# A linear-attention scan and a rational feed-forward layer on one core: units of one batch, register scales, and half of the denominators summed by DMA

## The chip, the cores and the metric

The kernel runs on one core of a Trainium2 chip. The engines are TensorE (PE in the profile, with PEld for its weight loads), VectorE (DVE), ScalarE (ACT), GpSimd (POOL) and SyncE (SP, which here only issues DMAs). The metric is device time in microseconds (us); the median of several runs is compared.

## The reference

Inputs q, k, v and f_logit have the shape [batch 4, heads 8, tokens 768, dim 48]. The first half is a recurrence with a gate for each key dimension; the second half is a feed-forward layer with a rational activation on 3072 tokens of width 8 x 48 = 384.

```python
f = 1 / (1 + exp(-f_logit))
for t in range(768):
    state = f[:, :, t, :, None] * state + outer(k[:, :, t], v[:, :, t])
    y[:, :, t] = q[:, :, t] @ state
x = y laid out as [3072, 384]
h = x @ w_in                                    # d_ff 2048
P = a0 + a1*h + a2*h*h + a3*h*h*h
Q = 1 + |b0|*|h| + |b1|*h*h + 1e-6
out = (P / Q) @ w_out
```

## The kernel before

The work is cut into 12 units of 256 tokens. A unit is two blocks of 128 tokens, one of each of two batches; a block stands on 64 partitions, two successive tokens (index i) to a partition. Twelve units are six chunks of 128 tokens times two pairs of batches, and the state of a pair is carried from chunk to chunk.

For the attention part of unit n the steps are, by their names in the code: `ld` (loads of f, k, q on SP's queue, of v with a cast to bf16 on POOL's queue, L185 to L195, two DMAs for an array, one per batch), `ef` and `ls` (exp and ln on ScalarE, L279 and L284: the log of the gate), `cs` (its running sum over the tokens by matmuls with triangular matrices, L294), `A` (exp of plus and minus that sum, L304 and L306, the one for q with a per-partition bias), `xa` (product with q and k on VectorE, L311), `T` and `Te` (transposes on TensorE and their copy out of PSUM, L322 and L330), `sc` and `mk` (scores, and their masking on VectorE, L343 and L351), `vm` (a copy of parts of v on POOL, L358), `ya` (the product with the carried state, and the next state in PSUM, L364 to L400), `yb` (scores times v, L364), `ye` (copy of y to the tile xT, L420), `ae` (exp of the last log sum, L425) and `st` (new state on VectorE, L429).

For the feed-forward part a unit has 16 tiles (m) of 128 hidden features by 256 tokens. The steps are: `h` (w_in products, L438), `hy` (copy of h to bf16 on ScalarE, L452), `sq` on VectorE (L456) or `sa` on ScalarE (L460) for h squared, `ab` (absolute value, L464), the denominator's sum either by `u` (two matmuls with the identity, L472, followed by `ln`, L480), or by `zd` (a DMA with addition issued on POOL, L489) or `zv` (VectorE, L485), both followed by `lz` (ln, L496). `ex` (L504) makes exp(-ln Q) = 1/Q. The numerator is `p1` (L509), `p2` (L514), `pm` (L519), then `ta` (a DMA with addition issued on POOL, L523) or `tv` (the same on VectorE, L527); `gm` (L532) multiplies numerator and 1/Q. `o` (L539) is the w_out product, `oe` (L554) its copy out of PSUM, `so` (L548) the store, two DMAs.

The features are scaled beforehand so that the denominator is c*(|h'| + h'*h') + 1: the factor sig[0] enters through the bias of `A` for q, and c is sig[2], a per-partition pointer in `ln` and `lz`.

Every engine and every DMA queue runs its instructions in program order, and the program order is written out by hand in the string ORDER (L19 to L104): some 800 steps, one after the other, with PSUM slots @0 to @3 (two banks each) named where a step opens one. A step waits for its data and for the free slot; all that is behind it on the same engine waits too. The load tiles have three buffers each.

Before the change the units differ: units 0 and 1 have all denominators by `u` and use `tv`; `sa` takes 48 of the 192 tiles of h squared, `zd` 40 and `zv` 24 of the denominators' tiles, `u` 128.

Of the kernel before, what the change touches and what calls it, by code (L numbers as in the profile page):

```python
# [19 lines left out]
cz 1; ld 0 v; ab_; ld 0 q 2 4; cz 0; ld 0 f 2 4; cz 2; cb; ld 0 f 0 2; wi 0 4; ld 0 k 2 4; fa  # L20
ld 0 k 0 2; cz 3; fb; ld 0 q 0 2; ef 0 2 4; ls 0 2 4; vm 0 0; ef 0 0 2; ld 1 f; vm 0 1; ls 0 0 2; ca
wi 4 16; cs 0 2 4 @0; cc; cs 0 0 2 @1; A 0 0 2 4; A 0 1 0 2; xa 0 0 2 4; A 0 1 2 4; A 0 0 0 2
xa 0 1 2 4; ld 1 k; xa 0 1 0 2; T 0 2 4 @1; xa 0 0 0 2; ld 1 q; Te 0 2 4; ld 1 v; T 0 0 2 @0
sc 0 1 @1; Te 0 0 2; ef 1; ld 2 f; mk 0 1; sc 0 0 @0; ya 0 @2 @3; ls 1; mk 0 0; yb 0 2 4; ae 0
cs 1 @1; st 0; yb 0 0 2; A 1 1; A 1 0; ye 0; h 0 0 4 @2; hy 0 0 4; h 0 4 8 @1; wo 4 8; wo 12 16
h 0 12 16 @2; hy 0 4 8; xa 1 1; ld 2 k; wo 0 4; h 0 8 12 @3; sq 0 0 8; wo 8 12; hy 0 12 16; ld 2 q
ab 0 0 8; hy 0 8 12; xa 1 0; u 0 0 4 @2; ab 0 8 16; T 1 @3; vm 1 0; ln 0 0 4; p1 0 0 8; ld 2 v
u 0 4 8 @1; Te 1; ef 2; ld 3 f; p2 0 0 8; sc 1 1 @3; vm 1 1; ln 0 4 8; sc 1 0 @2; mk 1 1; ls 2
ya 1 @1 @0; mk 1 0; ex 0 0 8; cs 2 @3; sq 0 8 16; yb 1; A 2 1; pm 0 0 8; u 0 12 16 @2; ye 1
p1 0 8 16; ae 1; A 2 0; h 1 0 4 @1; tv 0 0 8; ln 0 12 16; ld 3 k; h 1 12 16 @3; hy 1 0 4; p2 0 8 16  # L30
gm 0 0 8; h 1 4 8 @2; hy 1 12 16; pm 0 8 16; u 0 8 12 @1; hy 1 4 8; xa 2 1; h 1 8 12 @3; ln 0 8 12
tv 0 8 16; o 0 0 0 4 @2; ex 0 8 16; ab 1 0 8; o 0 1 0 4; sq 1 0 8; o 0 0 4 8; ld 3 q; hy 1 8 12
o 0 1 4 8; xa 2 0; u 1 0 4 @1; gm 0 8 16; T 2 @3; ld 3 v; ln 1 0 4; st 1; o 0 1 8 12; o 0 1 12 16
Te 2; ef 3; ld 4 f; vm 2 0; u 1 4 8 @0; vm 2 1; ls 3; sq 1 8 16; sc 2 0 @3; ln 1 4 8; sc 2 1 @1
ld 4 k; o 0 0 8 12; mk 2 0; o 0 0 12 16; ex 1 0 8; cs 3 @0; mk 2 1; ld 4 q; ab 1 8 16; A 3 1
ya 2 @1 @3; p1 1 0 16; A 3 0; vm 3 0; oe 0 0 2 s; yb 2; ld 4 v; xa 3 1; u 1 12 16 @0; ae 2; ye 2
so 0 0 2; p2 1 0 16; u 1 8 12 @2; ef 4; ld 5 f; vm 3 1; ln 1 12 16; h 2 12 16 @1; pm 1 0 8; ls 4
ld 5 k; st 2; h 2 0 4 @0; hy 2 12 16; tv 1 0 8; ln 1 8 12; cs 4 @3; ld 5 q; xa 3 0; h 2 4 8 @1
hy 2 0 4; gm 1 0 8; sa 2 0 4; h 2 8 12 @2; ld 5 v; pm 1 8 16; hy 2 4 8; o 1 0 0 4 @0; hy 2 8 12
ab 2 0 8; o 1 1 0 4; vm 4 1; tv 1 8 16; A 4 0; o 1 0 4 8; vm 4 0; ld 6 f; sa 2 4 8; T 3 @2  # L40
p1 2 0 16; A 4 1; o 1 1 4 8; ld 6 k; ex 1 8 16; xa 4 0; u 2 4 8 @1; Te 3; u 2 0 4 @3; ld 6 q
ln 2 4 8; gm 1 8 16; sc 3 1 @2; ln 2 0 4; sc 3 0 @1; mk 3 1; o 1 0 8 12; ef 5; o 1 1 8 12; mk 3 0
ex 2 0 8; o 1 1 12 16; ya 3 @2 @3; xa 4 1; ld 7 f; pm 2 0 8; ef 6; yb 3; ae 3; ls 5; T 4 @1; ld 7 k
# [69 lines left out]
def kernel(  # L113
# [14 lines left out]
    C = 128  # L128
# [91 lines left out]
    def const_b():  # L220
        make_identity(nc, ident)
# [372 lines left out]
```

## Time and profile before

| | |
|---|---|
| median of 3 runs | 247.41 us (247.39 to 249.63) |
| span of the profiled execution | 244.1 us |
| busy PE, DVE, ACT, POOL | 214.6, 210.6, 204.8, 62.1 us |
| first and second write of xT (start) | 26.85, 42.70 us |
| DMA packets, bytes moved | 61342, 37.94 MB |
| landing of one accumulating DMA of 512 KB (median) | 6.1 us (gall), 6.2 us (z) |

The page gives the span of one profiled execution, from the first to the last instruction, not that execution's own time; the median is of other runs and contains 3.3 us more. Busy time is the union of an engine's instructions; TensorE's are pipelined, so its busy share says little about its peak. In the list of groups a line names source line, engine, operation, tiles written and read, shapes, count, busy time and mean duration, then the idle time before such instructions and what ended it. A landing is the time from the issue of a DMA to its completion.

### The profile page before, as it was taken

Reading aid. Unit: us, or ns where it says so; the run is one execution under the profiler, and the core shown is the slowest. Engines: PE = TensorE matmul, PEld = TensorE weight load, DVE = VectorE, ACT = ScalarE, POOL = GpSimd, SP = SyncE. Lnnn points to the kernel's source line nnn. Section 1 sums busy time; section 2 is a strip of 40 time slices with the busy share of each in tenths; the row PEclk is TensorE's granted clock in tenths of the full one; section 3 lists DMA queues with packets and bytes.
Section 4 is the critical chain, followed back from the end, with each engine's and each line's share of the span. In section 5 each row is a group of like instructions: output and inputs, shape, how many; then the busy total and the mean of one; then the engine's idle time right before and its main releaser. Section 6 shows DMA issues by size and latency. Waiting matters only on the chain.

```text
span 244.1 us, 7193 instructions
## 1 busy us (share of the span) xinstructions
PE 214.6 (88%) x3144; PEld 146.9 (60%) x3144; DVE 210.6 (86%) x233; ACT 204.8 (84%) x213; POOL 62.1 (25%) x98
## 2 busy tenths in 40 slices
PE   0228787999998999997999999999999999999991
PEld 0115564765774868665668577668568658666550
DVE  7427179999999999999979999999999998899740
ACT  2422568989999899999799999999999999999930
POOL 7953201500400344233071032242122102004110
PEclk9999997999999999999999999999999999999997
DMA  6999999980799999999989999678529746606972
GB/s 82 217 199 198 204 196 221 208 131 0 127 208 204 166 239 169 201 200 220 161 161 165 232 179 172 101 153 131 105 74 172 145 97 118 121 3 129 199 145 64
DMA packets 61342, 37.94 MB, mean 155 GB/s; under 512 B 52096, under 2 KB 57600, under 8 KB 61312
## 3 DMA queue, kind: packets, MB, share of 16 engines
q0 software_dynamic: 19424, 18.62, 49.3%
q1 hardware_dynamic: 41888, 18.88, 40.1%
q8 instruction: 24, 0.39, 0.7%
q14 instruction: 6, 0.05, 0.1%
HBM read 25.17 MB, written 4.72 MB: 122 GB/s over the span
## 4 chain that ended last, share of the span: by engine, by line
PE 42%; ACT 18%; DMA 13%; DVE 13%; SPq 7%; issue 5%; DVEq 0%; ACTq 0%
PE op L539 15%; PE hp L438 13%; DMA fn<-in_f_logit_dram 8%; SPq L194 7%; DMA gall<-hy 5%; PE u L472 5%; ACT hy L452 4%; DVE gall L532 3%; ACT qi L504 3%; ACT lq L480 3%; PE y L364 2%; PE tp L322 2%; DVE h L456 2%; DVE gall L509 2%; PE sc L343 2%
## 5 line engine op out<-in xcount | busy, mean ns | idle before, releaser
L438 PE MATMUL hp<-xT,w_in_sb 128*128 128x256 bf16 x576 | 67.9, 273 | 1.7 <-ACT xT L420 1.4
L539 PE MATMUL op<-w_out_sb,gall 128*128 128x384 bf16 x384 | 68.4, 326 | 0.9 <-DVE osb L554 0.7
L438 PEld LDWEIGHTS <-w_in_sb 128*128 128x128 bf16 x576 | 55.4, 98 | 11.5 <-issue 2.1
L452 ACT CAST hy<-hp 128x1024 bf16<-128x1024 f32 x48 | 48.5, 1021 | 5.7 <-PE hp L438 5.4
L539 PEld LDWEIGHTS <-gall 128*128 128x128 bf16 x384 | 36.3, 98 | 25.5 <-DVE gall L532 1.2
L504 ACT ACTIVATE qi<-lq 128x2048 bf16<-128x2048 f32 (+1 forms) x25 | 46.5, 1871 | 0.2
L523 POOL DMA_DIRECT2D gall<-hy x21 | 19.5, 960 | 83.6 <-ACT hy L452 14.8
L480 ACT ACTIVATE lq<-u,sig 128x1024 f32<-128x1024 f32 x32 | 35.4, 1134 | 1.2 <-PE u L472 1.1
L532 DVE TENSOR_TENSOR gall<-gall,qi 128x2048 bf16<-128x2048 bf16 (+1 forms) x25 | 29.5, 1182 | 4.1 <-DMA gall<-hy 4.0
L351 DVE TENSOR_TENSOR scm<-sc,mask 128x1024 bf16<-128x1024 f32 x24 | 28.7, 1217 | 1.6 <-PE sc L343 1.6
L519 DVE TENSOR_TENSOR gall<-gall,h 128x2048 bf16<-128x2048 bf16 (+1 forms) x25 | 29.3, 1181 | 0.0
L194 POOL DMA_DIRECT2D vn<-in_v_dram x24 | 18.8, 801 | 27.0 <-issue 20.3
L456 DVE TENSOR_TENSOR h<-hy 128x2048 bf16<-128x2048 bf16 (+1 forms) x19 | 22.2, 1167 | 2.1 <-ACT hy L452 2.1
L294 PE MATMUL cs<-lsp,Ui 128*128 128x384 bf16 (+1 forms) x39 | 11.6, 359 | 12.5 <-ACT lsp L284 12.5
L358 POOL COPY vmp<-vn 128x128 bf16<-128x128 bf16 x24 | 10.7, 483 | 44.0 <-PE y L364 27.9
L279 ACT ACTIVATE fn<-fn 128x768 f32<-128x768 f32 (+1 forms) x13 | 10.7, 823 | 13.3 <-DMA fn<-in_f_logit_dram 13.3
L472 PE MATMUL u<-h,ident 128*128 128x512 bf16 x64 | 19.5, 387 | 0.0
L472 PEld LDWEIGHTS <-ident 128*128 128x128 bf16 x128 | 12.2, 99 | 11.7 <-issue 0.7
L472 PE MATMUL u<-z,ident 128*128 128x512 bf16 x64 | 19.1, 379 | 0.0
L322 PE MATMUL tp<-ident,qkp 128*128 128x128 bf16 x192 | 13.7, 227 | 6.0 <-DVE qkp L311 4.6
L509 DVE TENSOR_SCALAR gall<-hy,a_sb 128x4096 bf16<-128x4096 bf16 (+2 forms) x15 | 17.0, 1142 | 1.6 <-ACT hy L452 1.6
L311 DVE TENSOR_TENSOR qkp<-qn,A 128x768 bf16<-128x768 f32 (+1 forms) x13 | 11.6, 892 | 7.4 <-DMA qn<-in_q_dram 4.1
(70 smaller groups left out, 283.3 us busy)
## 6 DMA issues: line engine op xcount, KB each, us to landing
gall<-hy POOLq DMA_DIRECT2D x19, 512.0 KB, 6.1
fn<-in_f_logit_dram SPq DMA_DIRECT2D x22, 192.0 KB, 7.2
kn<-in_k_dram SPq DMA_DIRECT2D x22, 192.0 KB, 6.9
qn<-in_q_dram SPq DMA_DIRECT2D x22, 192.0 KB, 6.8
out_dram<-osb SPq DMA_DIRECT2D x22, 192.0 KB, 3.7
z<-h POOLq DMA_DIRECT2D x5, 512.0 KB, 6.2
vn<-in_v_dram POOLq DMA_DIRECT2D x24, 96.0 KB, 8.0
w_out_sb<-in_moe_w_out_dram POOLq DMA_DIRECT2D x4, 384.0 KB, 15.9
```

What stands on the lines that cost most here:

```text
L194: eng.dma_start(out=s[what][R * j:R * j + R, hh].rearrange("p h i d -> p h (i d)"), in_=src[s["u"] * UB + j, hh, t0:t0 + C, :].rearrange(" ...
L351: nc.vector.tensor_mul(t, s["sc", g].rearrange("s r a i t -> s (r a) (i t)"), mb)
L438: nc.tensor.matmul(t[:, m - m0, :].rearrange("f (j t) -> f j t", j=UB), w_in_sb[:, kk, m * P:(m + 1) * P], s["x"][:, :, kk, :], start=(kk ...
L452: nc.scalar.copy(fl(big(s, "hy", "hy", 3), m0, m1), fl(s["hp", m0], 0, m1 - m0))
L456: nc.vector.tensor_mul(fl(big(s, "h2", "h2", 2), m0, m1), fl(s["hy"], m0, m1), fl(s["hy"], m0, m1))
L472: nc.tensor.matmul(t[:, m - m0:m - m0 + 2, :].rearrange("p m t -> p (m t)"), ident, fl(src, m, m + 2), start=(x == 0), stop=(x == 1))
L480: nc.scalar.activation(fl(s["lq", g], m0 - 8 * g, m1 - 8 * g), fl(s["u", m0], 0, m1 - m0), AF.Ln, scale=sig[:, 2:3], bias=1.0 + 1e-6)
L504: nc.scalar.activation(fl(s["qi", g], m0 - 8 * g, m1 - 8 * g), fl(s["lq", g], m0 - 8 * g, m1 - 8 * g), AF.Exp, scale=-1.0)
L509: nc.vector.tensor_scalar(fl(big(s, "g", "gall", 3), m0, m1), fl(s["hy"], m0, m1), a_sb[:, 3:4], a_sb[:, 2:3], op0=ALU.mult, op1=ALU.add)
L519: nc.vector.tensor_mul(fl(s["g"], m0, m1), fl(s["g"], m0, m1), fl(s["h2"], m0, m1))
L532: nc.vector.tensor_mul(fl(s["g"], m0, m1), fl(s["g"], m0, m1), fl(s["qi", g], m0 - 8 * g, m1 - 8 * g))
L539: nc.tensor.matmul(s["op"][:, j, 0:DM], s["g"][:, m, C * j:C * j + C], w_out_sb[:, m, :], start=(m == 0), stop=(m == KF - 1))
```

## The change

- A unit is now 256 successive tokens of one batch (three chunks times four batches). Its two halves j = 0 and 1 follow each other in time, so the state goes through `sv j`, `st j` and `yi j` half by half: `sv 0`, `st 0`, then `sv 1` and `yi 1` with the new state. Each half has its own state tile.
- A load is one DMA of 128 partitions for an array instead of two of 64. w_in is loaded by three DMAs for a range of columns instead of four.
- The scales sig[0] and sig[2] are loaded into two registers of ScalarE (`fr`) once. `ln`, `lz` and the new `ye` use the registers; `ye` now multiplies by sig[0], and `A` for q has no bias any more.
- Every unit uses `u` and `ln` for tiles 0 to 8, and `zd` and `lz` for tiles 8 to 16. `sa`, `zv` and `tv` are not used any more: `sq` does all of h squared, `ta` all of the numerators' last sums.
- Only the padding of qkp, lsp and vmp is zeroed. The coefficient loads are issued on ACT's queue (b) and later on SP's (a).
- `p1` and `p2` always take 16 tiles. `oe` and `so` always take a whole unit, the last one too.
- ORDER is written anew. w_out and the first quarter of w_in are loaded later, among the first two units' steps.

In numbers of steps (or of tiles m for the steps of the feed-forward part):

| step | before | after |
|---|---|---|
| sq, sa (tiles) | 144, 48 | 192, 0 |
| u with ln (tiles) | 128 | 96 |
| zd, zv (tiles) | 40, 24 | 96, 0 |
| ln, lz (instructions) | 32, 8 | 24, 12 |
| ta, tv (tiles) | 160, 32 | 192, 0 |
| p1, p2 (instructions each) | 15 | 12 |
| st (instructions) | 10 of 128x768 | 20 of 128x384 |
| DMAs for v, and for each of f, k, q | 24, and 26 | 12, and 13 |

The core of the diff:

```diff
-            c, u = divmod(n, NU)
-            units[n] = dict(c=c, u=u, qk=qkp[n % 2], ls=lsp[n % 2], vm=vmp[n % 2], st=states[u])
+            c, b = divmod(n, B)
+            units[n] = dict(c=c, b=b, qk=qkp[n % 2], ls=lsp[n % 2], vm=vmp[n % 2], st=states[b])
...
-        for j in range(UB):
-            eng.dma_start(out=s[what][R * j:R * j + R, hh].rearrange("p h i d -> p h (i d)"),
-                          in_=src[s["u"] * UB + j, hh, t0:t0 + C, :].rearrange("h (p i) d -> p h (i d)", i=2))
+        eng.dma_start(out=s[what][:, hh].rearrange("p h i d -> p h (i d)"),
+                      in_=src[s["b"], hh, t0:t0 + NT, :].rearrange("h (p i) d -> p h (i d)", i=2))
...
+    def coef_r():
+        for i in (0, 2):
+            regs[i] = nc.scalar.alloc_register(f"sig{i}")
+            nc.scalar.reg_load(regs[i], sig[0:1, i:i + 1].bitcast(U32))
...
-        if x == 0:
-            nc.scalar.activation(t, src, AF.Exp, scale=-1.0, bias=sig[:, 3:4])
-        else:
-            nc.scalar.activation(t, src, AF.Exp, scale=1.0)
+        nc.scalar.activation(t, src, AF.Exp, scale=1.0 if x else -1.0)
...
+    def yi(n, j, sl=None):
+        s = unit(n)
+        y_open(s, sl)
         for kk in range(KD):
+            for a in range(HP):
+                ymm(s, j, a, kk, s["st"][j][:, a, 32 * kk:32 * kk + 32], s["T"][:, 0, :, a, R * j:R * j + R])
...
-        nc.scalar.copy(t.rearrange("p j k t -> p j (k t)"), s["y"][:, :, 0:KD * C])
+        if eng == "s":
+            return nc.scalar.mul(t.rearrange("p j k t -> p j (k t)"), s["y"][:, :, 0:KD * C], regs[0])
...
-        nc.vector.tensor_mul(s["st"], s["sv"], _at(s["ae"], [[1, UB], [UB, HP], [0, 2 * D]]))
+        return nc.vector.tensor_mul(s["st"][1 - j], s["sv"][:, j], _at(s["ae"], [[UB, HP], [0, W]], j))
...
-                             scale=sig[:, 2:3], bias=1.0 + 1e-6)
+                             scale=regs[2], bias=1.0 + 1e-6)
```

The beginning and the end of the new ORDER:

```
cz 0; ab_ b a; ld 0 f 2 4; ld 0 v; ld 0 f 0 2; cz 3; cu 1; ld 0 k 0 2; cz 1; cu 0; ld 0 q 2 4; fa
ld 0 q 0 2; wi 4 16; ef 0 2 4; ld 0 k 2 4; cz 2; ef 0 0 2; ls 0 0 2; fr; ls 0 2 4; cs 0 2 4 @1; vm 0 1
ld 1 f; cs 0 0 2 @0; ld 1 v; A 0 1 0 2; A 0 1 2 4; xa 0 1 0 2; A 0 0 2 4; vm 0 0; A 0 0 0 2; ci; xa 0 0 2 4
ld 1 k; xa 0 0 0 2; xa 0 1 2 4; T 0 0 2 @2; T 0 2 4 @1; Te 0 0 2; Te 0 2 4; sc 0 0 @2; ld 1 q; sv 0 0 @0
ef 1; cm; sc 0 1 @3; mk 0 0; ls 1; ae 0; cs 1 @1; ab_ a s; mk 0 1; A 1 1; st 0 0; A 1 0; xa 1 1; sv 0 1
yb 0 0 2 @1; ld 2 f; yi 0 1; xa 1 0; yb 0 2 4; ld 2 q; wi 0 4; ye 0 s; fb; T 1 @3; st 0 1; h 0 12 16 @0
...
lz 11 8 16; o 10 0 12 16; gm 11 0 8; o 10 1 8 12; o 10 1 12 16; ex 11 8 16; o 11 0 0 4 @3; o 11 0 4 8
oe 9 0 2 s; o 11 1 0 4; gm 11 8 16; oe 10 0 2 s; o 11 1 4 8; so 9 0 2 s; o 11 1 8 12; o 11 0 8 12
so 10 0 2 s; o 11 1 12 16; o 11 0 12 16; oe 11 0 2 s; so 11 0 2 s
```

## The prediction

> **What bounds the kernel now.** I read the page first, for the busy shares and the slices.
>
> ```profile
> span 244.1 us, 7193 instructions
> PE 214.6 (88%) x3144; PEld 146.9 (60%) x3144; DVE 210.6 (86%) x233; ACT 204.8 (84%) x213; POOL 62.1 (25%) x98
> ...
> PE   0228787999998999997999999999999999999991
> ...
> DVE  7427179999999999999979999999999998899740
> ACT  2422568989999899999799999999999999999930
> ```
>
> Three engines lie within 10 us of each other, and from the eighth slice on all three stand at 8 or 9. So no single engine bounds this kernel: a gain needs work off all of them, or a shorter beginning, where the digits are low. Second view: busy time in stretches, cut at the first and second write of xT (26.85 and 42.70 us) and by who leads the chain. Columns: length, then busy PE, PEld, DVE, ACT, POOL with instructions in brackets, TensorE clock, DMA share, GB/s.
>
> ```profile
> 0.00:26.85 26.85, 9.81 (x166) 6.51 (x167) 13.54 (x37) 8.62 (x15) 15.29 (x35) 1.00 1.08 177
> 26.85:42.70 15.85, 12.48 (x215) 8.82 (x215) 11.74 (x13) 10.96 (x12) 1.77 (x5) 0.92 1.34 207
> 42.70:112.00 69.30, 67.51 (x1080) 47.28 (x1079) 68.21 (x67) 66.06 (x72) 17.34 (x22) 0.99 1.03 170
> 112.00:178.00 66.00, 64.19 (x994) 44.62 (x994) 63.74 (x61) 63.89 (x64) 17.39 (x25) 1.00 0.91 158
> 178.00:229.00 51.00, 50.81 (x642) 34.40 (x640) 47.70 (x49) 49.51 (x48) 9.49 (x12) 1.00 0.58 114
> 229.00:244.10 15.10, 9.82 (x56) 5.25 (x56) 5.70 (x9) 5.75 (x6) 0.84 (x1) 0.91 0.59 124
> ```
>
> The reader is to see 42.7 us in which no engine is full and the DMA share is above 1 (packets overlap, so a share over 1 is possible; 1.38 at 205 to 211 GB/s is the highest in any 10 us). Third view: the chain of waits up to 45 us, and the timeline of ScalarE there.
>
> ```profile
> 5.15 5.41 DMA fn<-in_f_logit_dram
> ...
> 23.63 13.86 DMA fn<-in_f_logit_dram
> ```
>
> ```profile
> 21.82 0.84 ACT L279 ACTIVATE fn<-fn 128x768 f32<-128x768 f32 x1 [7.87 <-DMA fn<-in_f_logit_dram]
> ...
> 26.85 0.80 ACT L420 CAST xT<-y 128x768 bf16<-128x768 f32 x1
> ```
>
> The beginning is a matter of loads: ScalarE stood 7.87 us for unit 1's f. Fourth view, groups of instructions with shapes apart, for the prices (count, busy us, mean ns):
>
> ```profile
> L480 ACT ACTIVATE lq<-u,sig 128x1024 f32<-128x1024 f32 x32 | 35.4, 1134 | 1.2 <-PE u L472 1.1
> L456 DVE TENSOR_TENSOR h<-hy 128x2048 bf16<-128x2048 bf16 x17 | 20.8, 1223 | 2.1 <-ACT hy L452 2.1
> L496 ACT ACTIVATE lq<-z,sig 128x2048 f32<-128x2048 bf16 x8 | 16.2, 2024 | 0.0
> L460 ACT ACTIVATE h<-hp 128x1024 bf16<-128x1024 f32 x12 | 12.6, 1053 | 0.2 <-PE hp L438 0.2
> L304 ACT ACTIVATE A<-cs,sig 128x768 f32<-128x768 f32 x11 | 10.1, 921 | 0.9 <-PE cs L294 0.9
> L306 ACT ACTIVATE A<-cs 128x768 f32<-128x768 f32 x11 | 9.1, 828 | 1.8 <-PE cs L294 1.8
> ```
>
> **The sum is made against the span, 244.1.** The median shown is 247.41, so 3.3 us lie outside the span; they are added at the end.
>
> **Up to the first xT (now 26.85).** In the new order f of unit 0 is SP's first transfer (the two coefficient loads, 0.39 and 0.42 us of issue, leave SP's head, one for ACT's queue), each array of a unit is one transfer in place of two, and w_out and a quarter of w_in go behind on POOL. What must land for the first xT: f, k, q of unit 0 and f of unit 1 (4 x 0.39 MB), v (0.2 MB written) and three quarters of w_in (1.2 MB), 2.95 MB; at 200 GB/s that is 14.8 us, so unit 1's f lands near 16 and not at 21.8. From that landing to xT took 26.85 - 21.82 = 5.0 us; first xT near 21. The serial half-unit chain (sv, ae 0.19, st 0.56 by the 128x384 product of L311, then yi) adds some 1 us to unit 0, and the two register loads have no row: between nothing and two table loads (2 x 1.28), taken as two short DMA issues, 0.8. The wait for unit 1's f covers both; with that cover gone they cost 1.8 here. Memsets of the padding alone (4.3 us of memset now) end before data lands: nothing.
>
> **Up to the second xT (now 42.70).** It came 15.85 us after the first, with 2.4 us of ScalarE waiting for unit 2's f. The new steps between the two hold 9.5 us of PE, 7.4 of DVE, 6.7 of ACT. Ends: 11 us after the first if only PE counts; 18.7 if DMA runs as full as now and three accumulating transfers come on top. I take 14.5, near the present row: second xT at 35.5, **-7.2** (ends -10.7 and -3.0).
>
> **From the second xT on (now 201.4 us).** Counting the steps behind `ye 1` in both orders:
> - PE: 20 tiles fewer through u, four matmuls at 0.86 us in the chain, so 0.215 a tile: -4.3; two half-unit inter steps fewer, -0.5. Other counts are equal, state and inter products only split. Busy 192.3 goes to 187.5.
> - DVE: sq takes the 48 tiles of sa and 8 more, +8.4; pm and ab +1.6 (more of unit 0 lies behind); tv -4.9, zv -3.6 (4 and 3 x 1.215); xa -0.95, osb -0.6; state update 16 x 0.56 for 9 x 0.95, +0.4; rest -0.2. Sum +0.1: 185.4 stays.
> - ACT: sa -12.6; ln 6 fewer at 1.134, -6.8; lz four more at 2.024, +8.1; one ex, +1.8; osb -0.5; the pointer to a scale or bias gone from 46 instructions at 0.09 (921 - 828 ns on the same shape), -4.1. Busy 185.2 goes to 171.1. If the register costs what the pointer did, 175.2, still under the others. ye takes a register scale too: 0 to 1 us in all, covered likewise.
>
> Now PE had 9.1 us idle in this part, DVE 16.0: 7.6 of it after its last product, 4.0 waiting for accumulating transfers, the rest for PE and ACT. So PE's floor is 187.5 + 9.1 = 196.6, DVE's 185.5 + 7.6 + 4.0 = 197.1. Two queues equally full do not interleave without loss; I take 198.5, **-2.9** (ends -6, if the gaps shrink, and +1, if DVE keeps its 16.0).
>
> The tail: the last store is one of 192 KB behind one 0.81 us copy, now halves of 0.48 and 96 KB. Landing medians are 3.7 and 2.2: +1.8 if all shows, 0 if the last copies run in PE's shadow as now; **+1**.
>
> **Accumulating transfers.** zd goes from 5 to 12 and ta from 21 (two of half size) to 24. They are hidden if they land before the consumer: landing is 6.1 us (min 3.9, max 10.1), and the new order puts between the last producer and lz or gm at least 6.7 us of the fullest engine's work, mostly 8 to 14; only `ta 11 0 8` has 5.9. At 6.1 nothing is late but 0.2; at 8.5 the shortfalls add up to 8.5 us, at 9 to 13. I take **+1** (0 to +12), nearer the median: by 165 us the loads are nearly done and landings fall to 4.8. POOL's own issues (0.9 us each, +10) replace 12 merged v loads (0.8 each); POOL is busy 25%. But POOL issues in order: a ta that waits for p2 holds the v load and the vm copies written behind it, and yb waits for these.
>
> The Trainium skill speaks against this part: the page SBUF — State Buffer (section A bandwidth-pool intuition that's wrong) says that a POOL-issued DMA can take 3.1 us in place of 0.62 while VectorE holds a shared port. By that rule ten more accumulations under a full DVE would cost an estimated 10 x 2.5 = 25 us if all stood on the path, and the time would be near 263. The trace differs in what sets the landing: medians of 6.9 and 10.1 for z and gall at 87 to 100 us and 4.8 at 170 to 190, with DVE full in both; what changed is the load traffic. I keep the rows' +1.
>
> **Sum:** 244.1 - 7.2 - 2.9 + 1 + 1 = 236.0 in the span, 239.3 with the 3.3 around it.
>
> **Rivals.**
> 1. *The transfers come late* (the other side). Accumulations begin at once; now the first is issued at 87 us. From 30 to 90 us the packets' time was about 63 us over 60; nine more at 2.9 us of 16 engines (128 packets of 4 KB, 362 ns each) make 89, a share of 1.48, above the 1.38 seen. For: 10.1 us landings where loads ran. Against: 50 to 60 had a share of 0.34, so loads can shift. It decides at a typical landing of 8.6 us, where the shortfalls eat the 9 us of gain; at 9.5 they are about 18: near 256, range 250 to 262.
> 2. *The loads decide the beginning anyway*: merged transfers carry the same 384-byte packets, start gain 3.0, and DVE keeps its 16.0 us of idle: 244.1 - 3.0 + 1 + 1 + 1 + 3.3 = 247.4; 243 to 249.
> 3. *The relief works in full*: starts 10.7 earlier, -6 behind, tail and transfers nothing: 230.7; 229 to 233.
> 4. *Register scales save nothing*: ACT +4.1, covered as above, 239.3 unchanged.
>
> **How the numbers follow.** Forecast 0.56 (own range 233 to 244), rival 1 0.15, rival 2 0.23, rival 3 0.06; rival 4 goes with any. The predicted time is the likeliest's, 239.3. The range 231 to 250 leaves out rival 1 but its lowest edge and part of rival 3. One per cent (244.9 to 249.9) is about what a measurement can tell. Faster: 0.56 + 0.06 + a quarter of rival 2 (0.06) = 0.68. Same: 0.17 of rival 2. Slower: 0.15.
>
> **What would show it.** First xT near 21 and second near 35; no 7.87 us wait of ACT for f. DVE at 97% or more from 36 to 225 us. ln near 1.04 us, lz near 1.93, both A forms near 0.83. Waits of DVE for gall<-hy and of ACT for z<-h together under 6 us. Wrong if a third xT, not the second, shows the early loss given back, if landings exceed 8.6, or if PE waits for vm or v behind POOL.

## The result: slower by about one per cent, not faster

The kernel after takes 250.09 us (median of 4 runs, 249.32 to 250.42), the kernel before in the same session 247.97: a ratio of 1.0113, 95% interval 1.0068 to 1.0157. Forecast were 239.3 us and a range of 231 to 250. The profiled execution of after has a span of 247.6 us and took 249.32. Medians are of all runs; runs more than 1.5% above the fastest of their kernel count as disturbed and enter no ratio, which leaves k_both below one run of ten (242.98 us) and a_zd two of four (246.29 and 248.50 us), so that neither has an interval, and the profiles of a_w and k_both are of disturbed runs.

The first lines of its page and its slices:

```profile
span 247.6 us, 7084 instructions
PE 216.8 (88%) x3128; PEld 151.8 (61%) x3128; DVE 205.9 (83%) x232; ACT 190.4 (77%) x197; POOL 64.4 (26%) x94
...
PE   0307898979899998989999999999999999999990
...
DVE  5217568999998969979979999999899898999630
ACT  3402376998995986996988998997965997799961
```

ScalarE was relieved as planned (204.8 to 190.4 us). TensorE, which was to lose 4.8 us behind the second xT, has 2.2 more over the whole span: from the nineteenth slice on it stands at 9 in all but the last, while ScalarE has slices at 5, 6 and 7. The stretches, cut at the first and second write of xT (28.81 and 41.09 us here), in the same columns as for before:

```profile
0.00:28.81 28.81, 10.49 (x180) 7.55 (x181) 11.86 (x37) 8.27 (x14) 10.09 (x25) 1.00 1.17 174
28.81:41.09 12.28, 12.23 (x218) 9.39 (x218) 9.29 (x14) 7.21 (x9) 2.63 (x3) 1.00 1.09 234
41.09:112.00 70.91, 65.39 (x1032) 46.66 (x1032) 65.71 (x68) 62.63 (x66) 19.67 (x27) 1.00 1.04 189
112.00:178.00 66.00, 66.00 (x919) 45.89 (x917) 63.26 (x64) 59.84 (x62) 18.39 (x22) 1.00 1.00 198
178.00:218.00 40.00, 39.79 (x649) 29.25 (x648) 38.28 (x39) 30.68 (x30) 8.35 (x12) 1.00 0.67 116
218.00:247.60 29.60, 22.90 (x138) 13.02 (x136) 17.48 (x16) 21.75 (x18) 5.24 (x5) 0.99 0.78 160
```

From 112 to 218 us TensorE is busy for 105.8 of 106 us; before had 64.2 of 66.0 from 112 to 178 us. The gain up to the second xT is 42.70 - 41.09 = 1.6 us, and from there to the end the kernel needs 247.6 - 41.09 = 206.5 us where before needed 201.4.

ScalarE's timeline at the beginning answers to the 7.87 us wait of before:

```profile
21.50 0.84 ACT L267 ACTIVATE fn<-fn 128x768 f32<-128x768 f32 x1 [10.70 <-DMA fn<-in_f_logit_dram]
...
28.81 0.81 ACT L411 ACTIVATE xT<-y 128x768 bf16<-128x768 f32 x1 [2.56 <-PE y L355]
```

Unit 1's f is used at 21.50 us, 0.3 us earlier than before, and ScalarE stands for it even longer. The groups that the register scales touch (count, busy us, mean ns):

```profile
L477 ACT ACTIVATE lq<-u 128x1024 f32<-128x1024 f32 x24 | 24.1, 1031 | 3.1 <-PE u L466 2.9
L491 ACT ACTIVATE lq<-z 128x2048 f32<-128x2048 bf16 x12 | 23.1, 1921 | 0.0
...
L291 ACT ACTIVATE A<-cs 128x768 f32<-128x768 f32 x22 | 17.0, 817 | 4.5 <-PE cs L282 4.2 <-ACT hy L446 0.3
```

These came as forecast: 1031 ns for 1134, 1921 for 2024, both A at 817. (The diff has three changes that the list above leaves out: the two halves of `lq` and of `qi` have one buffer each where two went in turn, `alast` has two, and the transposes take k ahead of q. In after's groups on ScalarE that write `lq` or `qi` the idle time is 3.1 us for `ln`, 2.9 of it for TensorE's `u`, and 0.2 us in all for `lz` and `ex`, so the buffers cost little or nothing.)

What did not come as forecast stands in TensorE's groups of the attention products, in before:

```profile
L364 PE MATMUL y<-scm,vn 64*32 64x128 bf16 x384 | 10.5, 236 | 0.0
L364 PE MATMUL y<-scm,vmp 64*32 64x128 bf16 x384 | 8.6, 235 | 0.0
...
L395 PE MATMUL sv<-vn,qkp 64*64 64x48 bf16 x320 | 4.6, 192 | 0.0
```

and in after:

```profile
L355 PE MATMUL y<-scm,vn 64*32 64x128 bf16 x384 | 14.9, 226 | 1.0 <-ACT A L291 0.7 <-ACT hy L446 0.2
L355 PE MATMUL y<-scm,vmp 64*32 64x128 bf16 x384 | 12.3, 224 | 0.0
L403 PE MATMUL sv<-vn,qkp 64*64 64x48 bf16 x320 | 9.0, 192 | 0.0
```

The same numbers of instructions, of the same shapes and even a shorter mean, occupy TensorE for longer: the busy time is the union of overlapping matmuls, and fewer of them overlap. TensorE's timeline shows it at one place. Columns: start, length of the group up to the end of its last matmul, line, operation. First one unit of before:

```profile
79.27 0.44 PE L395 MATMUL sv<-vn,qkp 64*64 64x48 bf16 x32
79.64 0.35 PE L400 MATMUL sv<-ind,lsp 128*128 128x2 bf16 x8
79.92 0.25 PE L364 MATMUL y<-scm,vn 64*32 64x128 bf16 x8
79.99 0.29 PE L364 MATMUL y<-scm,vmp 64*32 64x128 bf16 x16
80.10 0.36 PE L364 MATMUL y<-scm,vn 64*32 64x128 bf16 x16
80.24 0.35 PE L364 MATMUL y<-scm,vmp 64*32 64x128 bf16 x16
80.37 0.28 PE L364 MATMUL y<-scm,vn 64*32 64x128 bf16 x8
80.59 1.07 PE L322 MATMUL tp<-ident,qkp 128*128 128x128 bf16 x16
```

then half a unit of after:

```profile
69.00 0.24 PE L355 MATMUL y<-scm,vn 64*32 64x128 bf16 x4
69.06 0.28 PE L355 MATMUL y<-scm,vmp 64*32 64x128 bf16 x8
69.17 0.28 PE L355 MATMUL y<-scm,vn 64*32 64x128 bf16 x8
69.28 0.28 PE L355 MATMUL y<-scm,vmp 64*32 64x128 bf16 x8
69.40 0.23 PE L355 MATMUL y<-scm,vn 64*32 64x128 bf16 x4
69.56 0.82 PE L539 MATMUL op<-w_out_sb,gall 128*128 128x384 bf16 x4
...
70.47 0.43 PE L403 MATMUL sv<-vn,qkp 64*64 64x48 bf16 x16
70.84 0.34 PE L282 MATMUL cs<-lsp,Ui 128*128 128x384 bf16 x1
```

From start to the start of what follows, yb of a whole unit took 80.59 - 79.92 = 0.67 us for 64 products; half of it, 32 products, takes 69.56 - 69.00 = 0.56. The k times v products took 0.37 us for 32 and take 0.37 for 16 (70.84 - 70.47). In the code the four head pairs of yb write to four groups of 32 PSUM partitions and the two halves j read two groups of 64 rows, eight separate parts of TensorE's array; the new order works on two head pairs at a time, four parts. `sv j` uses two of four parts. The Trainium skill, page TensorEngine Tiling (Array Packing), section Key Properties, has the rule: different tiles execute in parallel, and a change of tiling mode drains the engine. By that rule alone half the tiles would take twice the time per product, an estimate of 12 x 0.67 = 8.0 us more for yb; by the rows it is 12 x (2 x 0.56 - 0.67) = 5.4, if all units stood like this one. In units 2, 5 and 7 the halves follow each other directly. In 5 and 7 they take 0.83 and 0.82 us together, and in unit 2 0.96, no more than the whole yb takes at that place in the experiment a_yb below (1.03). So some 4.4 us is nearer (9 x 0.45 and 0.3).

### The profile page after: what moved, and what is told of

Its sections match the earlier page's. It is cut to its first block, busy times and chain, and to the rows that moved or that the text cites. A ratio compares the mean times of both kernels' runs of the same rounds, so it can differ in the third digit from the quotient of the medians.

```text
span 247.6 us, 7084 instructions
## 1 busy us (share of the span) xinstructions
PE 216.8 (88%) x3128; PEld 151.8 (61%) x3128; DVE 205.9 (83%) x232; ACT 190.4 (77%) x197; POOL 64.4 (26%) x94
## 4 chain that ended last, share of the span: by engine, by line
PE 64%; DMA 11%; ACT 11%; issue 7%; DVE 3%; SPq 2%; ACTq 0%; POOLq 0%
PE hp L432 21%; PE op L539 17%; DMA fn<-in_f_logit_dram 7%; PE y L355 7%; PE u L466 5%; PE tp L312 4%; DMA gall<-hy 4%; PE cs L282 3%; PE sc L334 3%; ACT lq L491 2%; PE sv L403 2%; ACT qi L499 2%; ACT hy L446 2%; ACT lq L477 2%; SPq L190 2%
## 5 line engine op out<-in xcount | busy, mean ns | idle before, releaser
L499 ACT ACTIVATE qi<-lq 128x2048 bf16<-128x2048 f32 x24 | 45.9, 1919 | 0.2
L486 POOL DMA_DIRECT2D z<-h x12 | 13.2, 1099 | 76.8 <-DVE z L458 29.5
L531 DVE TENSOR_TENSOR gall<-gall,qi 128x2048 bf16<-128x2048 bf16 x24 | 29.2, 1219 | 4.2 <-DMA gall<-hy 2.4
L450 DVE TENSOR_TENSOR h<-hy 128x2048 bf16<-128x2048 bf16 x24 | 29.1, 1217 | 0.4 <-ACT hy L446 0.4
L518 DVE TENSOR_TENSOR gall<-gall,h 128x2048 bf16<-128x2048 bf16 x24 | 28.9, 1217 | 0.0
L477 ACT ACTIVATE lq<-u 128x1024 f32<-128x1024 f32 x24 | 24.1, 1031 | 3.1 <-PE u L466 2.9
L291 ACT ACTIVATE A<-cs 128x768 f32<-128x768 f32 (+1 forms) x26 | 18.7, 767 | 6.0 <-PE cs L282 5.8
L491 ACT ACTIVATE lq<-z 128x2048 f32<-128x2048 bf16 x12 | 23.1, 1921 | 0.0
L296 DVE TENSOR_TENSOR qkp<-kn,A 128x768 bf16<-128x768 f32 (+1 forms) x13 | 11.7, 900 | 13.2 <-DMA kn<-in_k_dram 7.9
L312 PE MATMUL tp<-ident,qkp 128*128 128x128 bf16 x192 | 14.6, 235 | 8.3 <-DVE qkp L296 5.6
L320 DVE COPY qkT<-tp 128x2048 bf16<-128x2048 bf16 (+1 forms) x13 | 14.8, 1138 | 5.1 <-PE tp L312 3.0
L312 PEld LDWEIGHTS <-qkp 128*128 128x128 bf16 x192 | 12.5, 105 | 10.1 <-DVE qkp L296 7.5
```

What stands on the lines that cost most here:

```text
L312: nc.tensor.transpose(t[:, x, i, p, :], s["qk"][:, x, i, 2 * p:2 * p + 2, :].rearrange("t h d -> t (h d)"), ident)
L450: return nc.vector.tensor_mul(fl(big(s, "h2", "h2", 2), m0, m1), fl(s["hy"], m0, m1), fl(s["hy"], m0, m1))
L477: nc.scalar.activation(fl(lq(s, g), m0 - 8 * g, m1 - 8 * g), fl(s["u", m0], 0, m1 - m0), AF.Ln, scale=regs[2], bias=1.0 + 1e-6)
L491: nc.scalar.activation(fl(lq(s, g), m0 - 8 * g, m1 - 8 * g), fl(s["z"], m0, m1), AF.Ln, scale=regs[2], bias=1.0 + 1e-6)
L499: nc.scalar.activation(fl(s["qi", g], m0 - 8 * g, m1 - 8 * g), fl(s["lq", g], m0 - 8 * g, m1 - 8 * g), AF.Exp, scale=-1.0)
L518: return nc.vector.tensor_mul(fl(s["g"], m0, m1), fl(s["g"], m0, m1), fl(s["h2"], m0, m1))
```

## The experiments

Theory after the result: TensorE's lost packing makes it the bound from the second xT on. Rivals: the transfers, ScalarE's or VectorE's queue, the clock. In the diffs `+` is the experiment. A ratio is to the kernel before, with its 95% interval.

**a_yb: yb in one piece, at the place of its second half.**

```diff
+        if a1 < HP:
+            return
         for i0 in range(2):
             for par, kk in PIECE:
-                for a in range(a0, a1):
+                for a in range(HP):
```

> The changed kernel, with the scores-times-v product of a unit (yb) not in two halves of two head pairs but whole, at the place of its second half. Theory: TensorE bounds the changed kernel from about 94 to 218 us, and half products keep only half of its sub-arrays busy (64 matmuls took 0.67 us before, two times 32 take 2 x 0.56 after), 0.45 us a unit, 5.4 us in all. It expects 4 to 5.5 us less than the 250.1 of the changed kernel: 244.5 to 246. Rival, late accumulating transfers: within 1 us of 250.1, since no transfer is touched. Rival, the beginning alone: within 1 us.

Measured 245.2 us (4 runs, 244.34 to 245.9), ratio 0.9895 (0.9819 to 0.9972). After's ratio less this one is 0.022, some 5.4 us, give or take 2. Groups of a_yb:

```profile
L355 PE MATMUL y<-scm,vn 64*32 64x128 bf16 x384 | 9.4, 229 | 0.2 <-DVE scm L342 0.2
L355 PE MATMUL y<-scm,vmp 64*32 64x128 bf16 x384 | 7.5, 228 | 0.0
```

The same work in 9.4 and 7.5 us of TensorE for 14.9 and 12.3. This alone undoes the slowdown. By how much the kernel is then faster than before is less sure: the 25 runs of before in that session spread from 244.17 to 248.85 us, and among runs with a mean clock of 0.995 or more a_yb has a median of 244.84 us (3 runs) and before 246.16 (12 runs), a ratio of 0.995.

Nor is all of the gain TensorE's. The two profiled spans differ by 5.0 us. Of these 2.4 lie between the second and the last xT (170.9 us in after, 168.5 here) and 2.5 ahead of the second xT (41.09 and 38.60 us). There unit 1's f came 1.4 us earlier, ahead of every step that the edit touches:

```profile
20.13 0.84 ACT L267 ACTIVATE fn<-fn 128x768 f32<-128x768 f32 x1 [9.85 <-DMA fn<-in_f_logit_dram]
```

In the eleven profiled executions with after's order of loads at the beginning (after itself, a_yb, a_sv, a_both, a_tail, a_zd and the five k runs below) this f is used at anything from 20.1 to 23.6 us.

**a_sv: the k times v products of both halves side by side in `sv 0`; only the state's product is left in `sv 1`.**

```diff
-        nc.tensor.matmul(s["sv"][:, j], ident, s["st"][j], start=True, stop=True, skip_group_check=True)
+        nc.tensor.matmul(s["sv"][:, j], ident, s["st"][j], start=(j == 0), stop=True, skip_group_check=True)
+        if j == 1:
+            return
...
-                for par in range(2):
-                    r = slice(R * j, R * j + R)
...
+                for jj in range(2 if two else 1):
+                    for par in range(2):
+                        r = slice(R * jj, R * jj + R)
```

> The changed kernel, with the products of k and v of both halves of a unit interleaved in one step at sv 0 (four sub-arrays instead of two), only the old state's part of the second half left at sv 1. Theory: a call of 16 products takes 0.36 us now, 32 in one burst took 0.37 before, so 8 pairs save 0.35 us each, 2.8 us, plus one change of matmul shape less for each: 246.5 to 248. Rivals (late transfers, beginning): 249 to 251.

Measured 246.22 us, 0.9946 (0.9896 to 0.9996): 0.017 under after's ratio, some 4.1 us, where the rows give 8 x 0.37 = 3.0 (the four units of the last chunk have no second `sv`). In the profiled execution (span 244.5) the trace credits `sv` with less: 2.3 of its 3.1 us lie ahead of the second xT, with unit 1's f at 20.18 us, and 0.8 behind it (205.7 us for 206.5), while TensorE's busy time there falls by 2.2 us, from 194.1 to 191.9.

**a_both: the two together.**

> Both of these edits of the changed kernel together. Theory: TensorE's time adds up, 7 to 9 us less than 250.1: 241 to 243.5, below the kernel before (about 248). If VectorE takes over as the bound half way, 244 to 246. Rivals (late transfers, beginning): 249 to 251.

Measured 246.74 us, 0.9929 (0.9871 to 0.9986), no better than either alone. TensorE's busy time from the second xT on falls from 194.1 to 190.7 with yb whole and to 189.0 with both, but the stretch takes 206.5, 204.0 and 204.3 us. The second relief shows in TensorE's busy time and not in the time; what bounds instead was not shown.

**b_yb and b_both: the loss put into the kernel before.** In b_yb `yb` runs as two halves of two head pairs, one right behind the other; in b_both `sv` also has all products of one half ahead of those of the other.

```diff
+        if a1 - a0 == HP:
+            yb(n, 0, 2)
+            yb(n, 2, 4)
+            return
```

> The kernel before, with only its scores-times-v products (yb) issued in two halves of two head pairs one right behind the other, nothing else changed: same 64 matmuls, same places, no further change of shape. Theory: 0.45 us more for 11 units, 4 to 5 us more than before (about 252 to 253), since TensorE is at 97 to 100% there too. If only the changes of matmul shape cost, not the idle sub-arrays: within 0.5 us of before.

> The kernel before, with yb in two halves of two head pairs back to back and with the products k times v of one half after those of the other. Theory (packing of TensorE's sub-arrays lost): the halves of yb alone gave a ratio of 1.007 to before; with the second, 3.5 us more by the rows and about half of it shown, 249 to 251 us, a ratio of 1.012 to 1.02. Rival (the second edit is hidden behind other queues): 1.005 to 1.009.

Measured 247.32 us, 1.0073 (1.003 to 1.0115) and 247.69 us, 1.0067 (1.003 to 1.0105). The sign is right, the size of the first less than half of the expected, and of the second edit nothing is seen. TensorE's timeline in b_yb says why the size is smaller:

```profile
80.48 0.24 PE L364 MATMUL y<-scm,vn 64*32 64x128 bf16 x4
...
80.66 0.32 PE L364 MATMUL y<-scm,vn 64*32 64x128 bf16 x12
...
81.31 1.07 PE L322 MATMUL tp<-ident,qkp 128*128 128x128 bf16 x16
```

With no other shape between the halves the unit's yb takes 81.31 - 80.48 = 0.83 us, not 2 x 0.56 (the group of 12 is the end of one half and the beginning of the other, overlapping). Over the eleven units that the edit splits that is 11 x 0.16 = 1.8 us, and 1.0073 is 1.8 us. So of the 0.45 us a unit in after, 0.16 is the price of half the parts and 0.29 that of a half that stands alone between matmuls of another shape. The rival named ahead of the run, that only changes of shape cost, left 0.5 us; it is wrong for the smaller part and fits the larger, in which the change of shape and the group's own beginning and end were not told apart. In b_both a unit's 32 products k times v take 0.52 us where they took 0.37, but TensorE's busy time from the second xT on is 193.9 us as in b_yb (before: 192.3); why that total does not show them stays open.

**a_zd: the twelve transfers of `zd` left out.**

```diff
-        nc.gpsimd.dma_start(out=fl(s["z"], m0, m1), in_=fl(s["h2"], m0, m1), accum_op=ALU.add)
+        pass
```

> The changed kernel with the twelve accumulating transfers of the denominator left out (the denominators of tiles 8 to 16 lack the square). It removes 12 x 2.9 us of the DMA engines' time and 13 us of POOL's queue. Theory (packing on TensorE, w_in at the beginning): within 1.5 us of 250. Rival, late transfers: 4 us or more below 250.

Measured 249.49 us (246.29 to 250.74), span 246.8 against 247.6. By the median and the span these twelve transfers are not the cause; four runs that spread this far do not exclude a share of 1 or 2 us. The 24 others (`ta`) were left out in no run. VectorE waits 2.4 us for them in all (gall<-hy), yet after's chain passes through one:

```profile
83.79 9.09 DMA gall<-hy
```

**a_w, a_yw, a_yw2: the beginning.** In after, w_in's first three quarters (three DMAs, issued at 4.16 us) compete with the first units' loads: from 10 to 20 us w_in's packets have 0.53 of the DMA engines' time and the 384-byte packets of f, k and q 0.39 (from 5 to 15 us, the stretch that the text below names for these figures, it is 0.40 and 0.50). A part of unit 0's k is used at 17.77 us only, after a wait of 6.20. In a_w that load stands behind unit 1's f; a_yw has yb whole besides; a_yw2 has yb whole and w_in in two halves, one early and one late.

```diff
-ld 0 q 0 2; wi 4 16; ef 0 2 4
+ld 0 q 0 2; ef 0 2 4
-ld 1 k; xa 0 0 0 2; xa 0 1 2 4
+ld 1 k; xa 0 0 0 2; wi 4 16; xa 0 1 2 4
```

> The changed kernel with its first load of w_in (three quarters, rows of 3072 bytes) issued later on POOL, behind unit 0's vm copies and the identity instead of ahead of them. Theory: the early start was lost because w_in's long packets take most of the DMA engines' time from 5 to 15 us (0.53 of a share against 0.39 for the 384-byte rows of f, k, q), so that the last part of unit 0's k lands at 17.8 and unit 1's f at 21.5. It expects that k to land before 12, f of unit 1 before 15, the first xT at 19 to 23 instead of 28.8, and 4 to 7 us less in all: 243 to 246. Rival: the loads of f, k, q are bound by their own queue whatever w_in does: f of unit 1 stays at 19 or later, and the time within 1 us of 250. Second rival: the first h now waits for w_in instead, and the gain stays under 2 us.

> The later w_in together with whole scores-times-v products. If the two losses are separate, both gains add: 239 to 242. If VectorE's queue bounds the part behind the second xT (same work there as before), the start's gain still adds in full, since it moves that whole part: 240 to 242; if the loads bound the middle too, 243 to 246.

> Whole scores-times-v products, and w_in in two halves: tiles 8 to 16 (which h needs first) at the early place, tiles 0 to 8 at the later one, instead of three quarters and one. Theory: up to the second xT the DMA engines are full and the sum of bytes decides, so less w_in ahead lets f of unit 1 land near 17 and the first xT near 22, and the second half of w_in is in time because h of tiles 4 to 8 comes third: second xT near 36 instead of 38.6, 2 to 3 us below the same kernel with the early three quarters: 242 to 243.5. Rival: the sum of bytes is the same until the second xT: within 1 us of 245.2.

Measured 249.32 us, 1.0074 (1.0027 to 1.0121); 247.48 us, 0.9963 (0.9907 to 1.0019); 245.76 us, 0.9966 (0.9924 to 1.0009). In a_w the first xT came at 21.1 us, the 21 of the forecast, and the second at 42.4. TensorE's timeline there:

```profile
21.02 1.07 PE L312 MATMUL tp<-ident,qkp 128*128 128x128 bf16 x16
29.24 0.39 PE L432 MATMUL hp<-xT,w_in_sb 128*128 128x256 bf16 x1 [7.15 <-DMA w_in_sb<-in_moe_w_in_dram]
```

The wait has moved from f to w_in. That the sum of the bytes sets what the beginning costs fits this, but it is argued, not shown: the order alone moves the second xT from 42.4 (a_w) to 38.8 (a_yw) and 37.4 us (a_yw2), the latter two with yb whole. a_yw2, which splits w_in, has the earliest of all, yet its ratio is not below a_yb's.

**a_ywf and a_wf: is it the clock?** While TensorE stands for w_in the granted clock falls. The stretches of a_w (first busy PE, at the end clock, DMA share, GB/s):

```profile
24.00:28.00 4.00, 0.00 (x0) 0.00 (x0) 0.00 (x0) 0.00 (x0) 0.00 (x0) 0.55 1.67 122
28.00:32.00 4.00, 1.56 (x6) 0.80 (x7) 0.00 (x0) 0.00 (x0) 0.00 (x0) 0.50 1.35 187
```

In a_yw it is 0.53 and 0.62 there. a_ywf and a_wf fill that stand with matmuls that compute nothing (100 and 110 of them):

```diff
+        if n == 0 and m0 == 12:
+            for _ in range(100):
+                nc.tensor.matmul(t[:, 0, 0:P], ident, ident, start=True, stop=True, skip_group_check=True)
```

> yb whole and w_in's first load later, as in a_yw, and 100 extra matmuls of the identity (128 columns, some 5.6 us at full clock) written into the slot of the first h product just before it, where TensorE otherwise stands for w_in from 21.4 to 27.8 us. They add work and compute nothing that is used. Theory (the stand itself lowers the granted clock, in a_yw to 0.53 and 0.62 from 24 to 32 us, and the lost clock is what takes the earlier beginning back): the clock stays at 1.00 there, mean clock near 0.99, 242 to 244.5 us, ratio 0.983 to 0.993. Rival (the clock is not what costs the gain; the sum of the bytes and the order behind do): 246.5 to 248.5 us, as a_yw, or more.

> Only w_in's first load later, as in a_w, with 110 extra matmuls of the identity (some 6.2 us at full clock) in the stand from 22.1 to 29.2 us. Theory (clock): mean clock from 0.972 to near 0.99, 245 to 247 us, 3 to 5 us under a_w (249.3). Rival (not the clock): 249 to 250 us.

In a_ywf the clock was held:

```profile
24.00:28.00 4.00, 2.56 (x47) 2.39 (x45) 0.00 (x0) 0.00 (x0) 0.00 (x0) 1.00 1.47 167
28.00:32.00 4.00, 4.00 (x69) 3.55 (x67) 0.23 (x1) 0.59 (x1) 0.00 (x0) 1.00 1.25 196
```

Ahead of 24 us the column is no guide: it says 1.00 there too, but the filling matmuls, all of one shape, show a change of rate, 29 in 2.9 us and then 71 in 4.0 (to 29.90, the start of the next group):

```profile
21.59 2.90 PE L434 MATMUL hp<-ident 128*128 128x128 bf16 x29
25.92 4.14 PE L434 MATMUL hp<-ident 128*128 128x128 bf16 x71 [1.44 <-issue]
```

The median of the mean clock over the runs went from 0.975 to 0.991 in a_ywf and from 0.972 to 0.988 in a_wf. The time did not go with it: 247.65 us, 0.995 (0.9898 to 1.0002) against 0.9963, and 250.43 us, 1.002 (0.9951 to 1.0088) against 1.0074. The second xT of a_ywf is at 39.6 us, that of a_yw at 38.8. The 3 to 5 us that the theory of the clock expected are not there; the intervals leave room for some 2 us in a_ywf and 3 in a_wf. It fits that the clock was low where TensorE stood for data anyway.

**a_best: yb whole, the later w_in, `sa` for tiles 0 to 8 of units 3, 5, 7 and 9 in place of `sq`, and three output copies on VectorE.** For each such unit n and each copy, in the order:

```diff
-hy n 0 4
+hy n 0 4; sa n 0 4
-hy n 4 8
+hy n 4 8; sa n 4 8
-sq n 0 8
-oe 8 0 2 s
+oe 8 0 2 v
```

> Later w_in, whole scores-times-v products, and two moves between VectorE and ScalarE: the squares of tiles 0 to 8 of units 3, 5, 7, 9 on ScalarE (4 x 1.13 us off VectorE, 8 x 0.92 onto ScalarE, which is busy 77%), and the copies of the last products of units 8, 9, 10 on VectorE (3 x 0.7 us off ScalarE's queue in the tail, where VectorE stands idle). Theory: VectorE bounds the middle and ScalarE the tail, so 3 to 6 us below the same kernel without the moves: 234 to 238. Rival: neither queue is the bound there, the moves give nothing: 239 to 242.

Measured 253.8 us, 1.0285 (1.0195 to 1.0375): a clear miss. The moves brought the busy totals of VectorE and ScalarE nearer to each other (204.1 and 195.3 us, in a_yw 205.8 and 190.3) and lost time; `sa` was placed right behind `hy` in ScalarE's line, but what of the moves costs how much was not taken apart by runs of their own.

**Which queue bounds? k_pe, k_dve, k_act, and later k_both and k_dy.** Each leaves work of one engine out of after: k_pe the w_out products of tiles 12 to 16, k_dve `pm` of tiles 8 to 16, k_act the output copies (`oe` returns ahead of its copy, and one zeroed tile is stored for all units), k_both the first two, k_dy the second with yb whole. The edits of k_pe and k_dve:

```diff
-        for m in range(m0, m1):
+        for m in range(m0, min(m1, KF - 4)):
...
-                             start=(s["on", j] == 1), stop=(s["on", j] == KF))
+                             start=(s["on", j] == 1), stop=(s["on", j] == KF - 4))
...
     def pm(n, m0, m1):
         s = unit(n)
+        if m0 == 8:
+            return
```

> The changed kernel with the w_out products of tiles 12 to 16 left out (96 matmuls of 0.163 us, 15.6 us of TensorE; the output lacks their part). Everything on the other engines stays. If TensorE alone bounds the changed kernel from the second xT on: 12 us or more below 250. If VectorE's queue lies just behind it: 4 to 7 us below, about what whole scores-times-v products gave. If neither is the bound: under 2 us.

> The changed kernel with the product with h squared left out of the numerator for tiles 8 to 16 (12 x 1.22 us, 14.6 us of VectorE; the numerator is wrong there). If TensorE alone is the bound: under 2 us below 250. If VectorE is: 9 us or more. If both lie together: 2 to 5 us.

> The changed kernel without the copies of the last product out of PSUM (12 x 0.81 us of ScalarE; zeros are stored). If ScalarE's queue bounds only the tail, some 2 to 3 us below 250 (the three copies after the last hy); if nowhere, under 1; if it paces the middle through the order of its queue, 5 or more.

> Leaves out both the w_out products of tiles 12 to 16 (15.6 us of TensorE) and pm of tiles 8 to 16 (14.6 us of VectorE), so the numerators of those tiles and the sums over them are not the reference's. Each left out alone gave at most 2 us. Theory (TensorE's queue bounds the stretch between the second and the last xT, and VectorE's lies 3 to 5 us behind it): together they give much more than the sum of the two, 236 to 240 us, where ScalarE's queue is next. Rival (neither queue bounds it; the waits from engine to engine in the written order do): 245 to 250 us.

> yb whole as in the first experiment, and pm of tiles 8 to 16 left out (numerators of those tiles not the reference's). Leaving pm out alone gained nothing, with TensorE as the bound. Theory: with 5 us less of TensorE's time the VectorE queue decided in the first experiment, so that now a part of the 14.6 us shows: 241 to 244 us. Rival (VectorE is nowhere the bound, TensorE still is): 245 to 246 us, as with yb whole alone.

| | us | ratio (interval) | second to last xT | last xT to end |
|---|---|---|---|---|
| after | 250.09 | 1.0113 (1.0068 to 1.0157) | 170.9 | 35.6 |
| k_pe | 246.93 | 1.004 (0.9984 to 1.0096) | 167.8 | 35.5 |
| k_dve | 254.03 | 1.0284 (1.0174 to 1.0394) | 174.9 | 35.6 |
| k_act | 245.56 | 0.997 (0.9914 to 1.0026) | 173.0 | 30.6 |
| k_both | 248.42 | none | 170.7 | 35.6 |
| k_dy | 251.55 | 1.0176 (1.0096 to 1.0256) | 172.0 | 35.6 |

Only k_act did what a single bounding queue would do, and only in the tail: 5.0 us less behind the last xT. k_pe takes 3.1 us off the middle for 15.6 us of TensorE's work, so TensorE alone does not bound it, against the theory at the head of this section. k_dve is 4 us slower with 14.6 us less of VectorE's work. Together the two gave 1.7 us by the median, and one run of ten 7.1 (242.98 us). That speaks against two queues that bound jointly and for the rival, the waits between engines, but no run isolates these. One such wait can be named. It ends in the product of q on VectorE (L296). The chain of k_both has at 83 us, as one piece:

```profile
83.32 9.68 DMA qn<-in_q_dram
```

and that of k_dve:

```profile
83.53 10.65 DMA qn<-in_q_dram
```

In after no wait for q appears there; its chain passes at 83.79 us through the accumulating transfer shown above, and that of a_yb through a load of f:

```profile
80.18 13.39 DMA fn<-in_f_logit_dram
```

So all four have a transfer of 9 us or more on their path at this place. From 92 to 113 us k_both moves 224 GB/s at a DMA share of 1.16; its unit there takes 21.1 us from xT to xT (after: 18.6). The relieved engine meets loads that land 10 us after their issue. The clock (0.98 in k_both, k_dve and k_pe) may take part; what holds k_both in the rest of its span was not settled.

**a_tail: yb whole, and three of the last output copies on VectorE.**

> yb whole as in the first experiment, and the last four output copies but the very last (units 8, 9 and 10; 0.8 us each) on VectorE in place of ScalarE. Leaving all output copies out took 4.9 us from the tail. Theory (ScalarE's queue sets the tail): 242 to 244 us. Rival (the copies on VectorE hold up the last products, or the last store sets the end): 245 to 247 us.

Measured 246.96 us, 1.0025 (0.9986 to 1.0063): no gain; from the last xT to the end it takes 36.4 us, not less. a_yb keeps the lowest ratio. The other kernels with yb whole and all the work (a_both, a_yw, a_yw2, a_ywf and a_tail, without a_best) lie between 0.9929 and 1.0025, so the 0.9895 of its four runs may flatter it.

## Why the prediction was wrong, point by point

- **Failed: "Other counts are equal, state and inter products only split", costed at nothing.** TensorE's busy time behind the second xT was to go from 192.3 to 187.5 us and went to 194.1, 6.6 more. The split was counted in instructions, which are equal; in the rows their time depends on how many parts of the array work side by side and on what stands around them. Behind the second xT yb, which falls under the equal counts, costs 0.45 us more in seven units and 0.3 together in units 5 and 7, 3.5 us, and eight more calls of `sv` at 0.37 cost 3.0: 6.5 in all. The runs bear this out: yb whole takes 3.4 us off this busy time, `sv` with six pairs 2.2 (6 x 0.37), both together 5.1, and yb halved in before adds 1.5 (ten units x 0.16 = 1.6). A row of before could have warned: unit 0 there already had yb in halves, and the half at 22.89 us took 0.97 us for 32 products where the whole of unit 1 took 0.98 for 64 at 41.58, both in stretches in which these matmuls ran slower than later.
- **The floor behind the second xT**: 198.5 forecast, 206.5 measured. It splits into busy time (194.1 for 187.5, +6.6), gaps (12.4 for the 9.1 taken over from before, +3.3), less the 1.9 that was added for imperfect interleaving. The chain between the second xT and 213 us, by line, in after and then in a_yb:

```profile
by line: PE hp L432 24.9%; PE op L539 23.4%; PE u L466 7.8%; PE y L355 7.8%; issue 6.0%; DMA gall<-hy 5.3%; PE tp L312 4.5%; PE sc L334 3.2%; PE cs L282 3.2%; PE sv L403 2.7%; ACT hy L446 2.2%; PE sv L393 1.4%; ACT lq L477 1.1%; ACT lq L491
```

```profile
by line: PE hp L434 15.1%; PE op L541 12.9%; DMA fn<-in_f_logit_dram 7.8%; DVE scm L342 6.2%; issue 6.1%; DVE h L452 5.4%; DVE gall L533 4.9%; PE u L468 4.2%; DMA gall<-hy 4.1%; DVE gall L520 3.8%; DVE qkp L296 3.5%; PE y L355 3.5%; DVE hy 
```

  In after nearly four fifths of it are TensorE's lines; with yb whole VectorE and a load come in. Even so a_yb needs 204.0, not 198.5: taking before's gaps as gaps of the new order was too hopeful. Of the 8.0 us by which the floor was missed the lost packing, where it is taken back, gives 2.5 us of time (a_yb) or 2.2 (a_both); which waits of the new order make up the rest stays open.
- **VectorE**: 185.5 forecast, 184.7 measured. Right; but it was busy for 178.5 of 189 us from 36 to 225 us (94%), not 97%.
- **ScalarE**: 171.1 forecast, 174.9 measured; every price of the register scales is right, 3.8 us of the count are not traced. It cost nothing on the path but in the tail.
- **The beginning**: -7.2 forecast, -1.6 measured. The bytes were right and their order wrong: all 2.95 MB were to land by 16 us at 200 GB/s, but from 10 to 20 us after moved 175 GB/s, and f of unit 1 shared the engines with w_in. In a_w f came as forecast and w_in was late. 12.3 us from the first to the second xT (14.5 taken) gave 2.2 back. Rival 2, the loads decide the beginning, described it better: 3.0 there, 1.6 measured. Both stand in executions in which unit 1's f can land a microsecond or two earlier or later.
- **Transfers**: +1 forecast; leaving out the twelve `zd` gave 0.8 us of span. Nothing speaks against it, though no run left out `ta`. The median landings stayed under the 8.6 us of rival 1, and VectorE's wait for gall<-hy is 2.4 us in all. The 25 us that the forecast estimated from the Trainium skill's page SBUF — State Buffer, section A bandwidth-pool intuition that's wrong (but worth ruling out), are not seen: an issue on POOL takes 0.96 us for gall and 1.10 for z on average.
- **Tail**: +1 forecast, 35.6 for 34.4 us from the last xT to the end: +1.2. The size is right; the reason given, the larger last store and copy, was not tested by itself, and k_act shows that ScalarE's copies reach into the tail.
- **What lies around the span**: 3.3 us were added; after's profiled execution took 249.32 us for its span of 247.6, 1.7 more. The rest was spread between executions, not a fixed part.

## What to carry to other kernels

Count TensorE's time by groups between changes of shape, not by instructions: where small matmuls share the array, halving a group may leave most of its time as it was (0.56 of 0.67 us here), and most of that loss comes where the half stands alone between other shapes (0.29 of 0.45). When three engines lie within a few per cent, price a change by the chain of the new order; taking some 15 us off each of two of them moved the median by under 2 us here. An early landing is worth something only if all that the next step needs comes early too, so look at all loads of the first steps together. And before a gain is put down to an edit, cut both traces at the same events: half of a_yb's lay ahead of the stretch that it was meant to relieve.

## What the runs showed of the hardware

- 64-row by 32-column matmuls of 128 columns: 64 on eight parts of the array 0.67 us, 32 on four parts 0.56, 64 as two such halves back to back 0.83. 64 by 64 with 48 columns: 32 on four parts 0.37 us, 16 on two parts 0.36 to 0.37, 32 as two such halves back to back 0.52.
- The granted clock follows TensorE's own stands: 0.55 and 0.50 from 24 to 32 us in a_w, in a stand from 22.1 to 29.2, 1.00 again from 36 us on, and 1.00 from 24 to 32 us when the stand was filled. Early in a trace the column can say 1.00 while matmuls run slower: in a_ywf one of the filling matmuls takes 0.10 us up to 24 us and 0.06 behind it. The Trainium skill, page TensorE: Matmul & The Clock Gate, Part 1, says that the clock is halved after an idle window of some 3.4 us and full after a busy one. The rows agree in kind; by the mean of 0.55 the clock of a_w halved at some 24.4 us (an estimate), 2.3 us into the stand. Over the 117 executions of before that were run beside the experiments, 1% less of mean clock went with 2.1 us more of span (correlation -0.81); which of the two follows from the other is not shown.
- An accumulating DMA of 512 KB landed in a median of 6.7 us (gall) and 6.5 us (z), with 24 and 12 of them; before it was 6.1 and 6.2 with 21 and 5.
